# Splitting the first batch of an attention-plus-MoE kernel into two query parts, and moving its loads

## The chip, the cores and the metric

The kernel runs on 1 core of one Trainium2 chip. The metric is device time in microseconds (us); lower is better. Time before: 294.08 us, the median of 3 runs (293.91 to 294.34). "Clock" is the TensorE clock granted by the throttle, 1.00 being full speed.

## The reference

Block-causal attention over 8 batches, 8 heads, 576 tokens, head size 64, followed by a maxout feed-forward layer on all 4608 tokens:

```python
scores = scale * q @ k^T                 # 576 x 576 per head, masked in blocks of 64
attn   = softmax(scores)                 # exp, divided by the row's sum
x      = (attn @ v) as (4608, 512)       # heads side by side
g      = maximum(x @ w1, x @ w2)         # 4608 x 1024
out    = g @ w_out                       # 4608 x 512, float32
```

All inputs are float32 in HBM. The kernel computes in bfloat16.

## The kernel before

Heads are handled in 32 pairs of two. Two pairs are one *group*, which is loaded, cast and transposed together: "q4" is the q of group 4, needed by pairs 8 and 9, and its transposes stand in pair 6's turn. The four pairs of batch 0 are done first. After that the MoE matmuls ("filler") of the tokens that are finished are mixed between the attention of the next pairs. The schedule is by hand: each engine runs its instructions in the order in which the program emits them.

```python
def load_qk(g, queues, gated=False):
    for nm, src, queue in (("q", q, queues[0]), ("k", k, queues[1])):
        raws[nm, g] = t = raw.tile([P, 2, RPP * D], FP32, name=f"{nm}raw")
        if gated:
            nc.gpsimd.memset(t[:, 0, :1], 0.0)   # holds the load until GpSimd gets here
        queue.dma_start(out=t[:], in_=...)       # 576 KB
...
def fill_of(s):                                  # MoE matmuls to mix into pair s
    if s >= NPAIR - LAG:
        return 27
    left = 10 - s if s < 10 else 4 - (s - 2) % 4
    return -(-max(0, ready() - KEEP) // left)
...
# batch 0, all 576 queries of a pair at once: exps of 1024, 1024, 1024 and 128 elements
for s in range(HP):
    burst_a(s); ...; burst_b(s); pool_work(s); ...
...
elif s == 3:                                     # in pool_work
    cast("q", 2, ((act, 0, RPP),))
    cast("k", 2, ((act, 0, RPP),))
    load_qk(4, (SP, SP), gated=True)             # BEFORE the casts of group 3
    for c in range(3): load_v(1, c)
    cast("q", 3, ((pool, 0, RPP),))
    cast("k", 3, ((pool, 0, RPP),))
    for c in range(3, NCH): load_v(1, c)
    load_wo(0, 4)
    load_wo(4, 4)
```

The one-column memset makes a load wait for GpSimd's place in its program. So the order of GpSimd's instructions is also the order in which q and k loads go out. `warm_up(n)` issues n matmuls of zeros, meant to keep TensorE's clock up (two runs below, q4_late_cold and q4_late_warm, test this).

The softmax here doesn't subtract the row's maximum and nothing guards it: scores larger than these inputs give would overflow.

Of the kernel before, what the change touches and what calls it, by code (L numbers as in the profile page):

```python
# [14 lines left out]
def kernel(  # L15
# [38 lines left out]

    SPAN = 512
    NSPAN = NTOK // SPAN

# [31 lines left out]
    def load_qk(g, queues, gated=False):  # L89
        b, u = divmod(g, GPB)  # L90
        for nm, src, queue in (("q", q, queues[0]), ("k", k, queues[1])):
            raws[nm, g] = t = raw.tile([P, 2, RPP * D], FP32, name=f"{nm}raw")
            if gated:
                nc.gpsimd.memset(t[:, 0, :1], 0.0)
            queue.dma_start(
                out=t[:],
                in_=src[b, 4 * u:4 * u + 4].rearrange(
                    "(s h) (p t) d -> (h p) s (t d)", h=2, t=RPP),
            )
# [35 lines left out]
    load_qk(2, (SP, SP))  # L135
# [9 lines left out]
    cast("q", 0, ((dve, 0, 6), (pool, 6, RPP)))  # L145
# [3 lines left out]
    cast("q", 1, ((pool, 0, RPP),))  # L149
    for c in range(3, NCH):  # L150
        load_v(0, c)
    load_w(0, 256)
    load_w(256, 256)
# [5 lines left out]
    def h_unit(i, f):  # L159
        if f == 0:  # L160
            g_tiles[i] = g_pool.tile([P, NFF, SPAN], BF16, name="g")
        g = g_tiles[i]
        t0 = i * SPAN
        ph = []
        for w_sb in (w1_sb, w2_sb):
            pt = ps_m.tile([P, SPAN], FP32, name="ps_h", tag="m")
            for c in range(NDM):
                nc.tensor.matmul(  # L168
                    pt[:], w_sb[:, c, f * P:(f + 1) * P], xT[:, c, t0:t0 + SPAN],
                    start=(c == 0), stop=(c == NDM - 1),  # L170
                )
                if c == NDM - 1:
                    if not ph:
                        h1 = h1_pool.tile([P, SPAN], BF16, name="h1")
                        nc.vector.tensor_copy(out=h1[:], in_=pt[:])  # L175
                    else:
                        nc.vector.tensor_max(g[:, f, :], h1[:], pt[:])  # L177
                    ph.append(pt)
                yield

    def y_unit(i, s):
        g = g_tiles[i]
        t0 = i * SPAN + s * P
        py = ps_m.tile([P, d_model], FP32, name="ps_y", tag="m")
        for f in range(NFF):
            nc.tensor.matmul(  # L186
                py[:], g[:, f, s * P:(s + 1) * P], wo_sb[:, f, :],
                start=(f == 0), stop=(f == NFF - 1),
            )
            if f == NFF - 1:  # L190
                y = y_pool.tile([P, d_model], FP32, name="y")
                nc.scalar.copy(out=y[:], in_=py[:])  # L192
                nc.sync.dma_start(out=out[t0:t0 + P, :], in_=y[:])
            yield

    def y_last(i, s):
        g = g_tiles[i]
        t0 = i * SPAN + s * P
# [17 lines left out]
    def moe():  # L216
        ny = SPAN // P
        for i in range(NSPAN):
            need = (i + 1) * SPAN
            for f in range(NFF):  # L220
                yield from ((need, 0) for _ in h_unit(i, f))
                if i > 1 and f % 2 == 0:
                    yield from ((need, 0) for _ in y_unit(i - 1, f // 2))
            if i == 0:
                for s in range(ny):
                    yield from ((need, 0) for _ in y_unit(0, s))
        for s in range(ny - 1):
            yield from ((NTOK, 0) for _ in y_unit(NSPAN - 1, s))
        yield from ((NTOK, 0) for _ in y_last(NSPAN - 1, ny - 1))


    needs = []
    for i in range(NSPAN):
        needs += [(i + 1) * SPAN] * (2 * NDM * NFF + (SPAN // P * NFF if i != 1 else 0))
    needs += [NTOK] * ((SPAN // P + 1) * NFF)
    moe_steps = moe()
    at = [0]

    def ready():
        n = at[0]  # L240
        while n < len(needs) and needs[n] <= done_tokens[0]:
            n += 1
        return n - at[0]

    def fill(n):
        for _ in range(min(n, ready())):
            next(moe_steps)
            at[0] += 1
# [43 lines left out]
    def mask(p, a0):  # L292
        nc.gpsimd.memset(aT_r[p % NA][BLK:, :, a0:a0 + BLK], 0.0)  # L293
# [23 lines left out]
    def av(p, ts):  # L317
# [11 lines left out]
        for gi, t in enumerate(ts):  # L329
            for hh in range(2):  # L330
                for c in range(t + 1):
                    a0 = CB[c] + t * P
# [12 lines left out]
    def x_out(g):  # L345
        b, u = divmod(g, GPB)
        xp = xps.pop(g)
        pe = ps_m.tile([P, 2, NCH, BLK], BF16, name="ps_xe", tag="m")
        po = ps_m.tile([P, 2, NCH - 1, BLK], BF16, name="ps_xo", tag="m")
        for s in range(2):  # L350
            for t in range(NCH):
                src = xp[:, t, s].rearrange("p a d -> p (a d)")
                nc.tensor.transpose(pe[:, s, t, :], src[:BLK], ident[:BLK, :BLK])  # L353
                if t < NCH - 1:
                    nc.tensor.transpose(po[:, s, t, :], src[BLK:], ident[BLK:, BLK:])
        dst = xT[:, 2 * u:2 * u + 2, b * S:b * S + NCH * P].rearrange(
            "p s (t h w) -> p s t h w", h=2, w=BLK)
        nc.vector.tensor_copy(out=dst[:, :, :, 0], in_=pe[:])  # L358
        nc.vector.tensor_copy(out=dst[:, :, :NCH - 1, 1], in_=po[:])  # L359
        if u == GPB - 1:  # L360
            done_tokens[0] = (b + 1) * S
# [13 lines left out]
    def pool_work(s):  # L375
        g, i = divmod(s, 2)
        if s == 0:
            load_w(512, 512)
            load_qk(3, (SP, SP), gated=True)
        elif s == 1 or s == 2:  # L380
            pass
        elif s == 3:
            cast("q", 2, ((act, 0, RPP),))
            cast("k", 2, ((act, 0, RPP),))
            load_qk(4, (SP, SP), gated=True)
            for c in range(3):
                load_v(1, c)
            cast("q", 3, ((pool, 0, RPP),))
            cast("k", 3, ((pool, 0, RPP),))
            for c in range(3, NCH):  # L390
                load_v(1, c)
            load_wo(0, 4)
            load_wo(4, 4)
        elif s == 4:
# [30 lines left out]
    for s in range(HP):  # L425
        burst_a(s)
        if s == 0:
            cast("k", 1, ((dve, 0, RPP),))
            warm_up(4)
        elif s == 1:  # L430
            transposes("k", 1, (dve, dve))()
            warm_up(2)
        elif s == 2:
            av(0, [0, 1])
            warm_up(2)
        else:
            av(0, [2, 3, 4])
        burst_b(s)
        pool_work(s)
        if s == 0:  # L440
            transposes("q", 1, (dve, dve))()
            warm_up(2)
        elif s == 1:
            warm_up(4)
        elif s == 2:
            warm_up(3)
    for p in (1, 2, 3):
        av(p, [0, 1])
        av(p, [2, 3, 4])
        if p == 2:  # L450
            x_out(0)
    x_out(1)

    x_due = []
    for s in range(HP, NPAIR):
        g, i = divmod(s, 2)
        if x_due:
            x_out(x_due.pop())
        n = fill_of(s)
        if s == HP:  # L460
            fill(6)
            cq = transposes("q", 2, (dve, act))
            ck = transposes("k", 2, (dve, act))
            cq()
            ck()
            fill(6)
# [8 lines left out]
        if s >= HP + LAG:  # L475
# [4 lines left out]
            if p % 2:  # L480
                x_due.append(p // 2)
        else:
# [10 lines left out]
    fill(len(needs))  # L493
# [36 lines left out]
```

## Time and profile before

| what | before |
|---|---|
| time | 294.08 us |
| span of the profiled run | 292.3 us |
| TensorE busy | 281.2 us, of which 10.7 us are matmuls of zeros |
| ScalarE, VectorE, GpSimd busy | 140.2, 181.9, 95.7 us |
| first MoE matmul | 27.11 us |
| scores of pair 5 / 7 / 10 start | 36.65 / 46.03 / 63.38 us |

The views are read in the prediction below.

### The profile page before, as it was taken

How to read it: one execution, taken by the hardware profiler on the slowest of the kernel's cores; microseconds unless marked ns; L12 is line 12 of the kernel's file. 1: busy time of each engine (PE TensorE's matmuls, PEld its weight loads, DVE VectorE, ACT ScalarE, POOL GpSimd, SP SyncE). 2: the span in 40 equal slices, each digit the busy share in tenths (PEclk: the TensorE clock that was granted, in tenths of full speed). 3: DMA queues.
4: the chain of work that ended last, by engine and by line, in shares of the span. 5: the costliest groups of instructions: out<-in, count | busy, mean ns of one | idle time of the engine just before them, and what ended most of it. 6: DMA issues, size and time to landing. Idle time of an engine off the chain costs nothing.

```text
span 292.3 us, 7455 instructions
## 1 busy us (share of the span) xinstructions
PE 281.2 (96%) x3116; PEld 141.0 (48%) x3116; DVE 181.9 (62%) x363; ACT 140.2 (48%) x200; POOL 95.7 (33%) x236
## 2 busy tenths in 40 slices
PE   8787999999999999999999999999999999999995
PEld 3345445445554454544454455454545544444443
DVE  6717677547986676666565656666665766464530
ACT  3883686686655555554545555545555000101112
POOL 2967536625644443144324532443111000000000
PEclk9999999999999999999999999999999999999999
DMA  7999999968923792568656594465110111011104
GB/s 265 288 182 295 224 183 172 234 150 166 200 34 142 97 212 46 199 73 201 82 200 72 116 168 153 76 61 65 40 38 37 38 69 41 36 72 38 72 36 144
DMA packets 56081, 36.65 MB, mean 125 GB/s; under 512 B 38768, under 2 KB 43376, under 8 KB 56048
## 3 DMA queue, kind: packets, MB, share of 16 engines
q0 software_dynamic: 41728, 7.87, 34.5%
q1 hardware_dynamic: 13760, 27.60, 27.8%
q10 hardware_dynamic: 560, 0.72, 0.7%
q8 instruction: 24, 0.39, 0.6%
q14 instruction: 9, 0.07, 0.1%
HBM read 34.60 MB, written 9.44 MB: 151 GB/s over the span
## 4 chain that ended last, share of the span: by engine, by line
PE 89%; ACT 4%; DVE 3%; DMA 2%; issue 1%; ACTq 0%
PE ps_h L168 43%; PE ps_y L186 20%; PE ps_o L333 11%; PE ps_s L282 8%; ACT aT L288 3%; PE ps_qT L265 2%; DMA qraw<-in_q_dram 2%; PE ps_kT L265 2%; PE ps_xe L353 2%; PE ps_w L254 1%; DVE xp L340 1%; PE ps_y L203 1%; DVE xT L358 0%; DVE qT L272 0%; DVE kT L272 0%
## 5 line engine op out<-in xcount | busy, mean ns | idle before, releaser
L168 PE MATMUL ps_h<-xT,w_sb 128*128 128x512 bf16 x576 | 139.6, 380 | 0.5 <-DVE xT L359 0.4
L288 ACT ACTIVATE aT<-ps_s 128x1024 bf16<-128x1024 f32 (+1 forms) x128 | 99.2, 832 | 53.5 <-PE ps_s L282 53.5
L168 PEld LDWEIGHTS <-w_sb 128*128 128x128 bf16 x576 | 51.8, 98 | 59.7 <-issue 6.1
L175 DVE CAST h<-ps_h 128x512 bf16<-128x512 f32 x72 | 49.7, 691 | 45.0 <-PE ps_h L168 43.9
L186 PE MATMUL ps_y<-wo_sb,g 128*128 128x512 bf16 x280 | 69.6, 379 | 0.0
L293 POOL MEMSET aT<- 64x128 bf16 x128 | 23.6, 200 | 120.7 <-ACT aT L288 120.5
L192 ACT COPY y<-ps_y 128x512 f32<-128x512 f32 x35 | 20.5, 587 | 83.9 <-PE ps_y L186 61.4
L177 DVE TENSOR_TENSOR g<-h,ps_h 128x512 bf16<-128x512 bf16 x72 | 49.3, 684 | 10.2 <-PE ps_h L168 10.2
L333 PEld LDWEIGHTS <-aT 128*128 128x128 bf16 x960 | 33.6, 98 | 14.9 <-DVE xp L340 8.4
L333 PE MATMUL ps_o<-vv,aT 128*128 128x65 bf16 x960 | 39.7, 194 | 0.9 <-DVE xp L340 0.4
L186 PEld LDWEIGHTS <-g 128*128 128x128 bf16 x280 | 25.4, 98 | 27.9 <-issue 3.2
L282 PE MATMUL ps_s<-qT,kT 64*128 64x64 bf16 (+4 forms) x384 | 34.5, 275 | 3.0 <-ACT aT L288 2.9
L109 POOL DMA_DIRECT2D vv<-in_v_dram x40 | 33.7, 848 | 0.3 <-issue 0.3
L340 DVE TENSOR_TENSOR xp<-ps_o,rec 128x256 bf16<-128x256 f32 x64 | 31.4, 491 | 2.2
L282 PEld LDWEIGHTS <-kT 64*128 64x128 bf16 x384 | 16.5, 94 | 18.9 <-issue 13.2
L339 DVE RECIPROCAL rec<-ps_o 128x4 f32<-128x4 f32 x64 | 11.8, 184 | 18.9 <-PE ps_o L333 18.8
L105 POOL CAST qn<-qraw 128x1152 bf16<-128x1152 f32 (+1 forms) x15 | 17.1, 1138 | 4.8 <-DMA qraw<-in_q_dram 4.7
L272 DVE COPY qT<-ps_qT 128x576 bf16<-128x576 bf16 x17 | 12.8, 757 | 5.3 <-PE ps_qT L265 4.1
L358 DVE COPY xT<-ps_xe 128x640 bf16<-128x640 bf16 x16 | 7.8, 490 | 12.4 <-PE ps_xe L353 12.1
L105 POOL CAST kn<-kraw 128x1152 bf16<-128x1152 f32 x13 | 14.9, 1145 | 1.9 <-DMA kraw<-in_k_dram 1.2
L272 DVE COPY kT<-ps_kT 128x576 bf16<-128x576 bf16 x17 | 12.8, 756 | 4.3 <-PE ps_kT L265 3.3
L254 PE MATMUL ps_w<-zeros 128*128 128x512 bf16 x36 | 10.7, 432 | 1.7 <-DVE zeros L132 1.2
(39 smaller groups left out, 102.9 us busy)
## 6 DMA issues: line engine op xcount, KB each, us to landing
qraw<-in_q_dram SPq DMA_DIRECT2D x16, 576.0 KB, 4.4
out_dram<-y SPq DMA_DIRECT2D x35, 256.0 KB, 2.1
kraw<-in_k_dram SPq DMA_DIRECT2D x15, 576.0 KB, 6.5
vv<-in_v_dram POOLq DMA_DIRECT2D x32, 128.0 KB, 5.8
w_sb<-in_moe_w_dram POOLq DMA_DIRECT2D x4, 256.0 KB, 8.1
w_sb<-in_moe_w_dram POOLq DMA_DIRECT2D x2, 512.0 KB, 16.9
wo_sb<-in_moe_w_out_dram POOLq DMA_DIRECT2D x2, 512.0 KB, 12.6
kraw<-in_k_dram ACTq DMA_DIRECT2D x1, 576.0 KB, 5.6
```

The lines of the kernel that those rows point to most:

```text
L105: copy(out=n[:, j0:j1], in_=t[:, j0:j1])
L109: nc.gpsimd.dma_start(out=vv_r[b % NV][:rows, c, :, :D], in_=v[b, :, c * P:c * P + rows, :].rearrange("h p d -> p h d"),)
L168: nc.tensor.matmul(pt[:], w_sb[:, c, f * P:(f + 1) * P], xT[:, c, t0:t0 + SPAN], start=(c == 0), stop=(c == NDM - 1),)
L175: nc.vector.tensor_copy(out=h1[:], in_=pt[:])
L177: nc.vector.tensor_max(g[:, f, :], h1[:], pt[:])
L186: nc.tensor.matmul(py[:], g[:, f, s * P:(s + 1) * P], wo_sb[:, f, :], start=(f == 0), stop=(f == NFF - 1),)
L272: copies[i](out=t[:, :S].rearrange("q (p j) -> q p j", j=RPP), in_=pts[i].rearrange("q j p -> q p j"),)
L282: nc.tensor.matmul(ps[:m, hh, col:col + w], kT[r, c * P:c * P + m], qT[r, q0:q0 + w], start=True, stop=True,)
L288: nc.scalar.activation(out=aT_r[p % NA][:m, :, a0:a0 + w], in_=ps[:m, :, :w], func=AF.Exp, scale=scale,)
L293: nc.gpsimd.memset(aT_r[p % NA][BLK:, :, a0:a0 + BLK], 0.0)
L333: nc.tensor.matmul(po[:, gi, hh, :], a[:, hh, a0:a0 + P], vv[:, c, h0 + 2 * hh, :], start=(mm == 0), stop=(mm == n_mm - 1),)
L340: nc.vector.tensor_mul(xp[:, ts[0]:ts[0] + n, :, p % 2], po[:, :, :, :D], rec[:, :n].to_broadcast([P, n, 2, D]),)
```

## The change

The intent is to start MoE work earlier. Batch 0 is done in two query parts: queries 0 to 383 of all four pairs first, then 384 to 575. The first 384 tokens are an MoE span of their own, the other 192 a second one; the later spans of 512 then start 64 tokens into an output tile, and those 64 columns of g are copied ("carried") from the span before. The head is written out by hand, and with it the loads are reordered: k2 is held back from the start, group 3's load goes behind the casts of group 2, the first half of w_out goes ahead of the casts of group 3, and group 4's load goes behind them. The core of the diff (cut; [...] marks the cuts):

```diff
+    QCUT = 384
[...]
-    NSPAN = NTOK // SPAN
+    spans = [(0, QCUT), (QCUT, S - QCUT)]
+    spans += [(t0, min(SPAN, NTOK - t0)) for t0 in range(S, NTOK, SPAN)]
[...]
-    load_qk(2, (SP, SP))
+    load_qk(2, (SP, None))
[...]
-    cast("q", 1, ((pool, 0, RPP),))
[...]
+    cast("k", 1, ((pool, 0, RPP),))
[...]
-        elif s == 3:
-            cast("q", 2, ((act, 0, RPP),))
-            cast("k", 2, ((act, 0, RPP),))
-            load_qk(4, (SP, SP), gated=True)
[...]
-    for s in range(HP):
-        burst_a(s)
[...]
+    burst_p1(0)
+    burst_p2(0)
[...]
+    load_qk(2, (None, SP), gated=True)
[...]
+    load_w(512, 512)
+    cast("q", 2, ((pool, 0, RPP),))
+    cast("k", 2, ((pool, 0, RPP),))
+    burst_q1(0)
[...]
+    mask_q(1)
+    load_qk(3, (SP, SP), gated=True)
+    for c in range(3):
+        load_v(1, c)
[...]
+    load_wo(0, 4)
+    fill(3)
[...]
+    cast("q", 3, ((pool, 0, RPP),))
+    cast("k", 3, ((pool, 0, RPP),))
+    load_wo(4, 4)
+    load_qk(4, (SP, SP), gated=True)
+    fill(3)
```

Group 4's load now comes after group 3's casts.

More of the change, by code (lines that the diff above doesn't have):

```diff
@@ L53, with a_col @@
     NCH = 5
-    SPAN = 512
-    NSPAN = NTOK // SPAN
+    QCUT = 384
+    def a_col(p, c, t):
+        if p >= HP:
+            return CB[c] + t * P
+        return {
+            0: (0, 768 - QCUT), 1: (512 - P, 960 - QCUT),
+            2: (384 - 2 * P, 1152 - QCUT), 3: (0, 1344 - QCUT), 4: (0, 1536 - 4 * P),
+        }[c][t * P >= QCUT] + t * P if (c, t) != (2, 4) else 1280
+    SPAN = 512
+    spans = [(0, QCUT), (QCUT, S - QCUT)]
+    spans += [(t0, min(SPAN, NTOK - t0)) for t0 in range(S, NTOK, SPAN)]
+    NSPAN = len(spans)
+    carry = [t0 % P for t0, _ in spans]
+    tiles = [(carry[i] + w) // P for i, (_, w) in enumerate(spans)]
     wpool = ctx.enter_context(tc.tile_pool(name="wpool", bufs=1))
@@ L91, in load_qk @@
         for nm, src, queue in (("q", q, queues[0]), ("k", k, queues[1])):
+            if queue is None:
+                continue
             raws[nm, g] = t = raw.tile([P, 2, RPP * D], FP32, name=f"{nm}raw")
@@ L144 @@
         nc.vector.memset(aT_r[r][:BLK, :, AW:], 0.0)
-    cast("q", 0, ((dve, 0, 6), (pool, 6, RPP)))
+    cast("q", 0, ((dve, 0, 7), (pool, 7, RPP)))
     cast("k", 0, ((act, 0, 5), (dve, 5, RPP)))
@@ L148 @@
         load_v(0, c)
-    cast("q", 1, ((pool, 0, RPP),))
-    for c in range(3, NCH):
-        load_v(0, c)
-    load_w(0, 256)
-    load_w(256, 256)
+    cast("k", 1, ((pool, 0, RPP),))
     done_tokens = [0]
@@ L160, in h_unit @@
         if f == 0:
-            g_tiles[i] = g_pool.tile([P, NFF, SPAN], BF16, name="g")
+            g_tiles[i] = g_pool.tile([P, NFF, SPAN + BLK], BF16, name="g")
+            if carry[i]:
+                end = carry[i - 1] + spans[i - 1][1]
+                nc.gpsimd.tensor_copy(
+                    out=g_tiles[i][:, :, :carry[i]],
+                    in_=g_tiles[i - 1][:, :, end - carry[i]:end])
         g = g_tiles[i]
-        t0 = i * SPAN
+        t0, w = spans[i]
+        m = carry[i]
         ph = []
@@ L168, in h_unit @@
                 nc.tensor.matmul(
-                    pt[:], w_sb[:, c, f * P:(f + 1) * P], xT[:, c, t0:t0 + SPAN],
+                    pt[:, :w], w_sb[:, c, f * P:(f + 1) * P], xT[:, c, t0:t0 + w],
                     start=(c == 0), stop=(c == NDM - 1),
@@ L174, in h_unit @@
                         h1 = h1_pool.tile([P, SPAN], BF16, name="h1")
-                        nc.vector.tensor_copy(out=h1[:], in_=pt[:])
+                        nc.vector.tensor_copy(out=h1[:, :w], in_=pt[:, :w])
                     else:
-                        nc.vector.tensor_max(g[:, f, :], h1[:], pt[:])
+                        nc.vector.tensor_max(g[:, f, m:m + w], h1[:, :w], pt[:, :w])
                     ph.append(pt)
@@ L182, in y_unit @@
         g = g_tiles[i]
-        t0 = i * SPAN + s * P
+        t0 = spans[i][0] - carry[i] + s * P
         py = ps_m.tile([P, d_model], FP32, name="ps_y", tag="m")
@@ L197, in y_last @@
         g = g_tiles[i]
-        t0 = i * SPAN + s * P
+        t0 = spans[i][0] - carry[i] + s * P
         w = d_model // 2
@@ L214, in y_last, with plan, h, y @@
                 yield
-    def moe():
-        ny = SPAN // P
+    units = []
+    def plan():
+        def h(i, f):
+            t0, w = spans[i]
+            units.append((h_unit(i, f), t0 + w, w / SPAN, 2 * NDM))
+        def y(i, s, last=False):
+            t0, w = spans[i]
+            if last:
+                units.append((y_last(i, s), t0 + w, 0.5, 2 * NFF))
+            else:
+                units.append((y_unit(i, s), t0 + w, 1.0, NFF))
         for i in range(NSPAN):
-            need = (i + 1) * SPAN
             for f in range(NFF):
-                yield from ((need, 0) for _ in h_unit(i, f))
-                if i > 1 and f % 2 == 0:
-                    yield from ((need, 0) for _ in y_unit(i - 1, f // 2))
-            if i == 0:
-                for s in range(ny):
-                    yield from ((need, 0) for _ in y_unit(0, s))
-        for s in range(ny - 1):
-            yield from ((NTOK, 0) for _ in y_unit(NSPAN - 1, s))
-        yield from ((NTOK, 0) for _ in y_last(NSPAN - 1, ny - 1))
-    needs = []
-    for i in range(NSPAN):
-        needs += [(i + 1) * SPAN] * (2 * NDM * NFF + (SPAN // P * NFF if i != 1 else 0))
-    needs += [NTOK] * ((SPAN // P + 1) * NFF)
-    moe_steps = moe()
+                h(i, f)
+                if i > 2 and f % 2 == 0 and f // 2 < tiles[i - 1]:
+                    y(i - 1, f // 2)
+            if i == 1:
+                for j in range(2):
+                    for s in range(tiles[j]):
+                        y(j, s)
+        n = tiles[-1]
+        for s in range(n):
+            y(NSPAN - 1, s, s == n - 1)
+    plan()
+    steps = [(u, need, cost) for u, need, cost, n in units for _ in range(n)]
     at = [0]
     def ready():
-        n = at[0]
-        while n < len(needs) and needs[n] <= done_tokens[0]:
+        n, total = at[0], 0.0
+        while n < len(steps) and steps[n][1] <= done_tokens[0]:
+            total += steps[n][2]
             n += 1
-        return n - at[0]
+        return int(total)
     def fill(n):
-        for _ in range(min(n, ready())):
-            next(moe_steps)
+        while n > 0 and at[0] < len(steps) and steps[at[0]][1] <= done_tokens[0]:
+            u, _, cost = steps[at[0]]
+            next(u)
+            n -= cost
             at[0] += 1
@@ L290, in exp, with mask, burst, burst_p1 @@
         )
-    def mask(p, a0):
-        nc.gpsimd.memset(aT_r[p % NA][BLK:, :, a0:a0 + BLK], 0.0)
+    def mask(p, a0, eng=None):
+        (eng or nc.gpsimd).memset(aT_r[p % NA][BLK:, :, a0:a0 + BLK], 0.0)
+    def burst(p, parts, a0):
+        u = ps_s.tile([P, 2, 512], FP32, name="ps_s", tag="s")
+        w = 0
+        for c, q0, n in parts:
+            scores(p, u, w, c, q0, n)
+            w += n
+        exp(p, u, w, a0)
+    def burst_p1(p):
+        burst(p, ((0, 0, QCUT), (2, 256, P)), 0)
+    def burst_p2(p):
+        burst(p, ((1, P, QCUT - P),), 512)
+    def burst_q1(p):
+        burst(p, ((0, QCUT, 192), (1, QCUT, 192), (2, QCUT, P)), 768)
+    def burst_q2(p):
+        burst(p, ((2, 512, BLK), (3, QCUT, 192), (4, 512, BLK)), 1280)
+    def masks_p(p, eng=None):
+        for a in (0, 384, 512):
+            mask(p, a, eng)
+    def mask_q(p, eng=None):
+        mask(p, 1344, eng)
     def burst_a(p):
@@ L331, in av @@
                 for c in range(t + 1):
-                    a0 = CB[c] + t * P
+                    a0 = a_col(p, c, t)
                     nc.tensor.matmul(
@@ L343, in av, with x_out @@
         )
-    def x_out(g):
+    def x_out(g, t0=0, t1=NCH):
         b, u = divmod(g, GPB)
-        xp = xps.pop(g)
-        pe = ps_m.tile([P, 2, NCH, BLK], BF16, name="ps_xe", tag="m")
-        po = ps_m.tile([P, 2, NCH - 1, BLK], BF16, name="ps_xo", tag="m")
+        xp = xps[g]
+        n = t1 - t0
+        n_odd = min(t1, NCH - 1) - t0
+        pe = ps_m.tile([P, 2, n, BLK], BF16, name="ps_xe", tag="m")
+        po = ps_m.tile([P, 2, n_odd, BLK], BF16, name="ps_xo", tag="m")
         for s in range(2):
-            for t in range(NCH):
+            for t in range(t0, t1):
                 src = xp[:, t, s].rearrange("p a d -> p (a d)")
-                nc.tensor.transpose(pe[:, s, t, :], src[:BLK], ident[:BLK, :BLK])
+                nc.tensor.transpose(pe[:, s, t - t0, :], src[:BLK], ident[:BLK, :BLK])
                 if t < NCH - 1:
-                    nc.tensor.transpose(po[:, s, t, :], src[BLK:], ident[BLK:, BLK:])
-        dst = xT[:, 2 * u:2 * u + 2, b * S:b * S + NCH * P].rearrange(
+                    nc.tensor.transpose(po[:, s, t - t0, :], src[BLK:], ident[BLK:, BLK:])
+        dst = xT[:, 2 * u:2 * u + 2, b * S + t0 * P:b * S + t1 * P].rearrange(
             "p s (t h w) -> p s t h w", h=2, w=BLK)
         nc.vector.tensor_copy(out=dst[:, :, :, 0], in_=pe[:])
-        nc.vector.tensor_copy(out=dst[:, :, :NCH - 1, 1], in_=po[:])
+        nc.vector.tensor_copy(out=dst[:, :, :n_odd, 1], in_=po[:])
         if u == GPB - 1:
-            done_tokens[0] = (b + 1) * S
+            done_tokens[0] = min(b * S + t1 * P, (b + 1) * S)
     LAG = 2
@@ L376, in pool_work @@
         g, i = divmod(s, 2)
-        if s == 0:
-            load_w(512, 512)
-            load_qk(3, (SP, SP), gated=True)
-        elif s == 1 or s == 2:
-            pass
-        elif s == 3:
-            cast("q", 2, ((act, 0, RPP),))
-            cast("k", 2, ((act, 0, RPP),))
-            load_qk(4, (SP, SP), gated=True)
-            for c in range(3):
-                load_v(1, c)
-            cast("q", 3, ((pool, 0, RPP),))
-            cast("k", 3, ((pool, 0, RPP),))
-            for c in range(3, NCH):
-                load_v(1, c)
-            load_wo(0, 4)
-            load_wo(4, 4)
-        elif s == 4:
+        if s == 4:
             pass
@@ L424 @@
     ck((1,))
-    for s in range(HP):
-        burst_a(s)
-        if s == 0:
-            cast("k", 1, ((dve, 0, RPP),))
-            warm_up(4)
-        elif s == 1:
-            transposes("k", 1, (dve, dve))()
-            warm_up(2)
-        elif s == 2:
-            av(0, [0, 1])
-            warm_up(2)
-        else:
-            av(0, [2, 3, 4])
-        burst_b(s)
-        pool_work(s)
-        if s == 0:
-            transposes("q", 1, (dve, dve))()
-            warm_up(2)
-        elif s == 1:
-            warm_up(4)
-        elif s == 2:
-            warm_up(3)
-    for p in (1, 2, 3):
-        av(p, [0, 1])
-        av(p, [2, 3, 4])
-        if p == 2:
-            x_out(0)
-    x_out(1)
-    x_due = []
+    cast("q", 1, ((dve, 0, RPP),))
+    burst_p1(0)
+    burst_p2(0)
+    warm_up(2)
+    masks_p(0)
+    load_w(0, 256)
+    load_qk(2, (None, SP), gated=True)
+    cq = transposes("q", 1, (dve, dve))
+    burst_p1(1)
+    ck = transposes("k", 1, (dve, dve))
+    for i in range(2):
+        cq((i,))
+        ck((i,))
+    burst_p2(1)
+    masks_p(1)
+    for c in range(3, NCH):
+        load_v(0, c)
+    warm_up(2)
+    burst_p1(2)
+    warm_up(2)
+    av(0, [0, 1, 2])
+    burst_p2(2)
+    masks_p(2, nc.vector)
+    load_w(256, 256)
+    warm_up(3)
+    burst_p1(3)
+    av(1, [0, 1, 2])
+    warm_up(2)
+    burst_p2(3)
+    masks_p(3, nc.vector)
+    load_w(512, 512)
+    cast("q", 2, ((pool, 0, RPP),))
+    cast("k", 2, ((pool, 0, RPP),))
+    burst_q1(0)
+    av(2, [0, 1, 2])
+    warm_up(2)
+    burst_q2(0)
+    av(3, [0, 1, 2])
+    x_out(0, 0, 3)
+    burst_q1(1)
+    warm_up(2)
+    burst_q2(1)
+    x_out(1, 0, 3)
+    mask_q(0)
+    mask_q(1)
+    load_qk(3, (SP, SP), gated=True)
+    for c in range(3):
+        load_v(1, c)
+    warm_up(1)
+    burst_q1(2)
+    transposes("q", 2, (dve, dve))()
+    fill(3)
+    burst_q2(2)
+    mask_q(2)
+    for c in range(3, NCH):
+        load_v(1, c)
+    load_wo(0, 4)
+    fill(3)
+    burst_q1(3)
+    transposes("k", 2, (dve, dve))()
+    av(0, [3, 4])
+    fill(3)
+    burst_q2(3)
+    mask_q(3)
+    cast("q", 3, ((pool, 0, RPP),))
+    cast("k", 3, ((pool, 0, RPP),))
+    load_wo(4, 4)
+    load_qk(4, (SP, SP), gated=True)
+    fill(3)
+    av(1, [3, 4])
+    fill(4)
+    x_due = [0]
     for s in range(HP, NPAIR):
@@ L457 @@
         if x_due:
-            x_out(x_due.pop())
+            x_out(x_due.pop(), 3 if s < HP + 2 else 0)
         n = fill_of(s)
-        if s == HP:
-            fill(6)
-            cq = transposes("q", 2, (dve, act))
-            ck = transposes("k", 2, (dve, act))
-            cq()
-            ck()
-            fill(6)
         burst_a(s)
@@ L481 @@
                 x_due.append(p // 2)
+        elif s == HP:
+            av(2, [3, 4])
+            fill(n_b)
+            av(3, [3, 4])
+            x_due.append(1)
         else:
@@ L492 @@
     x_out(NG - 1)
-    fill(len(needs))
+    fill(len(steps))
 _INS = ['q', 'k', 'v', 'moe_w1', 'moe_w2', 'moe_w_out']
```

## The prediction

> **What bounds the kernel now.** I read the page's busy shares and slices first, then busy time by stretch, then TensorE's instructions in order of time for the first 35 us, then the DMA issues one by one.
>
> ```profile
> PE 281.2 (96%) x3116; PEld 141.0 (48%) x3116; DVE 181.9 (62%) x363; ACT 140.2 (48%) x200; POOL 95.7 (33%) x236
> ...
> PE   8787999999999999999999999999999999999995
> ```
>
> TensorE is busy 96% of the span, and its row of slices is below 9 only in the first 29 us and at the very end. By stretch:
>
> ```profile
> 15.00:16.00 1.00, 1.00 (x10) 0.34 (x8) 0.00 (x0) 0.59 (x2) 0.96 (x6) 1.00 3.03 102
> 18.00:21.00 3.00, 2.75 (x39) 1.69 (x39) 0.46 (x2) 2.66 (x5) 1.03 (x7) 1.00 1.45 196
> 21.00:31.00 10.00, 7.25 (x172) 5.22 (x172) 7.19 (x20) 4.41 (x7) 7.25 (x13) 1.00 1.14 294
> 63.00:280.00 217.00, 216.91 (x2312) 107.67 (x2312) 140.62 (x268) 95.71 (x137) 58.92 (x148) 1.00 0.47 99
> ```
>
> (Columns: stretch, length, busy time of PE, PEld, DVE, ACT, POOL, granted clock, DMA share, GB/s.) From 63 to 280 us TensorE is busy 216.91 of 217 us at full clock. Nothing there can be saved by reordering; all matmuls that are needed are still needed. A gain can come only from the head, where "busy" deceives, because part of it multiplies zeros:
>
> ```profile
> 18.11 0.21 PE L282 MATMUL ps_s<-qT,kT 64*128 64x64 bf16 x2 [0.52 <-ACT aT L288]
> 18.25 0.82 PE L254 MATMUL ps_w<-zeros 128*128 128x512 bf16 x3
> ...
> 21.45 0.20 PE L282 MATMUL ps_s<-qT,kT 64*128 64x64 bf16 x2 [0.52 <-ACT aT L288]
> ...
> 27.11 0.60 PE L168 MATMUL ps_h<-xT,w_sb 128*128 128x512 bf16 x2
> 28.09 1.02 PE L168 MATMUL ps_h<-xT,w_sb 128*128 128x512 bf16 x4 [0.38 <-DVE xT L359]
> ...
> 36.65 0.61 PE L282 MATMUL ps_s<-qT,kT 64*128 64x512 bf16 x6
> ```
>
> (Start, duration, instruction, count, idle before and its releaser.) The first MoE matmul is at 27.11 us. Before it TensorE owns only batch 0's attention: 4 sets of transposes at 0.27, 4 pairs of scores at 0.54 + 0.35, 4 pairs of AV at 0.92, two output transposes at 0.3, in all 9.0 us. So about 18 us of the first 27.1 are idle or zeros. What TensorE waits for there is ScalarE's exps: 9.23 to 22.4 us, four exps in 3.00 us per pair, then 0.34 to 0.53 us of idle before the next pair.
>
> DMA is the second bound of the head: its share is above 1 from about 4 to past 40 us, up to 3.03. Landings, as issue start plus time to landing of each issue: q0 5.95, k0 6.35, q1 about 7.8, k1 9.35, q2 10.85, k2 12.6; the v chunks of batch 0 at about 13.4, 14.4, 15.4 (0 to 2), 18.1, 18.7; the first weight columns at 19.2 and 20.2, the second at 22.7 and 26.1, the last at 31.3 and 35.1; q3 24.6, k3 28.1.
>
> **What the Trainium skill says.** "ScalarE: Activation LUTs", What ACT_TABLE_LOAD costs: 0.833 ns per element and about 93 ns of overlap between neighbours. The trace agrees: 1022 ns for 1024 elements and 260 ns for 128 give 0.85 ns per element, and two in a row take 1.94 us, 0.92 from start to start. By that line an exp of 512 is 0.59 us and one of 640 0.70 us (estimates). "TensorE: Matmul & The Clock Gate", Wait — 56ns, not 53.3ns?: start to start is N/2.4 GHz plus about 2.5 ns, so splitting a 512-column matmul costs next to nothing. The trace: 8 matmuls of 512 in 1.90 us with the last one's 0.38, 217 ns each against 215.7. "DMA: Bandwidth & Descriptors", Queues, rings and completion order: each engine takes turns between the queues it has work for, by packet. The trace agrees in kind: q3 and k3, issued at 17.5 and 17.9 beside the weights, need 7.1 and 10.2 us, where q0 alone needed 5.2.
>
> **The change, part by part.** I count MoE work in units of one 512-column matmul (0.217 us).
>
> *Split of batch 0.* Scores cover queries 0-383 of all four pairs first (exps of 1024 and 512), then 384-575 (1024 and 640). ScalarE per pair: 1022 + 586 + 1022 + 695 ns less four overlaps, 2.95 us, as before; but MoE can start after four first parts (4 × 1.42 = 5.7 us of exps from 9.23) and not after 13 us. Two long exps no longer stand around a 0.26 one, so the 0.5 us hole per pair shrinks too.
>
> *Worked order of the head (estimates from the durations above; ScalarE, VectorE and buffers each in program order).* Nothing differs to 9.2. The q1 cast is now on VectorE, 8.7 to 10.0 (1.35 measured for k1), the k1 cast on GpSimd ends about 10.6. VectorE's four copies at 0.75 bring pair 2 at 12.0 and pair 3 at 13.4. The first AV of three chunks needs v chunk 2. Without k2 in front (576 KB at about 400 GB/s is 1.4 us) it lands at about 13.9 and not 15.4. TensorE would be there at 13.2, and its queue is in order, so the second exp of pair 2 waits too: a hole of about 1.2 us on ScalarE. Then exps of pair 3 from 15.6 to 17.2, AV of pair 3 about 18.3, VectorE's division to 19.3, output transposes after the second-part scores of pair 1 at about 19.8, xT complete at 20.6. First MoE matmul at about **20.9**, 6.2 us earlier than 27.11.
>
> *What then stands in its way.* The fills until the loop (3+3+3+3+3+4) are 19.5 units, 4.2 us; among them four AV tails (two later, inside the loop) at 0.56, scores, k2's transposes. I get the start of pair 4's scores at about 27.7 against 32.04. There only tokens 0-383 are released: 48 units less 19.5 leave 28, so the fill for pair 4 is (28-6)/6, 4 units, where before had 15. Pair 4 also needs q3, which is now loaded only after k2's cast and the second exp of pair 1: issued about 21.1, landed about 27.6, cast by 28.8, wanted at 28.6. Pair 5's scores start at about 32.6 against 36.65, so 4.05 us ahead, but 24 units are done where before had 27: 3 × 0.217 = 0.65 us are still owed. Net **3.4 us**.
>
> *Pairs 5 to 9.* After: 104 units are released by batch 0 (576 tokens), before 96 (512 tokens); 75 against 63 are filled in here. More filler does not cost anything in sum, as the total stays 864. Widths of 192 double VectorE's instructions: with 692 ns for 512 and 292 for 128 one of 192 is about 0.36, so a pair of tiles takes 0.72 against TensorE's 8 × 0.083 = 0.66: VectorE becomes the limit for some 5 us if nothing else is interleaved. Before has idle of its own there (0.18, 0.32, 0.31, 0.27 us). I take 0.2 us for this and for 64 more MoE instructions at about 3 ns.
>
> *The rest.* Eight copies of g on GpSimd (512 elements a partition, well under the 1.15 us of its 1152-element casts) on an engine at 33%: nothing. The last span is 448 wide, the final tiles and the output are as before: nothing.
>
> Sum: 294.08 - 3.4 + 0.2, about **290.8**; I put 290.6, since the wait for v is the term I most likely set too long.
>
> **Rivals.**
> 1. *The loads don't keep up.* The backlog moves nothing earlier by itself: all that is needed 4 us earlier must still pass engines at share 1 to 3. q3 issued 3.6 us later than before is the tightest, then q4, whose issue now stands behind k3's cast (about 33, where before it was 22.9): landed about 38.3, cast 39.5, wanted at about 40.4. For: the 7 to 10 us landings in this stretch. Against: the weights go out earlier, and before has 9 us of slack for q3. If q3 and q4 are each 1.5 us late: about 293.
> 2. *ScalarE alone sets the head.* If v is there in time and no exp waits, the first parts end at about 15.5, xT at 18.3, and the gain grows by about 2 us: about 288.5. For: the new order never lets three long exps stand behind one buffer. Against: the v chunks have 1.0 us spacing and 6.6 us to landing.
> 3. *The gain is hidden anyway.* If the earlier MoE start only replaces filler later, because pairs 4 to 9 are bound by ScalarE (3.64 us per pair) or VectorE, pairs with 4 units stay idle: about 292 to 293. Against: before's pairs 5 to 9 take 5.3 us each, well over 3.64, so they absorb filler.
>
> **Range and chances.** My sum has one well-founded term (exps before MoE, 13 to about 6 us) and three waits of 1 to 2 us each that could go either way; together about 2 us each side: 288.3 to 292.9. Faster by over 2% means under 288.2, a gain of 5.9 us, nearly all of the earlier start without any new wait: 0.10. Slower needs 6 us of new waits: 0.02.
>
> **What would show it.** First MoE matmul near 20.9 us; TensorE idle before the first AV released late, with ScalarE's hole of about 1.2 us after pair 2's first exp; q3's cast ending near 28.8; pair 5's scores near 32.6; TensorE again without idle after about 62 us, its busy time lower by little, and all later stages the same. I am wrong if the loop starts later than 29 us or the stretch from 30 to 62 us shows more than 1.5 us of new idle (loads late), or if pair 5 starts before 31 (ScalarE alone).

## The result, and the profile after

| | before | after |
|---|---|---|
| time, median | 294.21 us (293.91 to 294.96, 4 runs) | 297.15 us (296.58 to 297.41, 4 runs) |
| clock, mean over the span | 0.998 | 0.987 to 0.994 |
| first MoE matmul | 27.11 us | 20.74 us |
| scores of pair 5 start | 36.65 us | 32.83 us |
| scores of pair 7 start | 46.03 us | 49.27 us |

The ratio is 1.0093 (95% interval 1.0068 to 1.0119). Ratios are the mean time of one kernel's fast runs over that of the other's fast runs of the same rounds, so they are not quite the ratio of the medians quoted. The change made the kernel 0.9% slower. I had predicted 290.6, in a range of 288.3 to 292.9.

The page of the changed kernel, busy shares and slices of 7.4 us each:

```profile
PE 279.4 (95%) x3158; PEld 146.8 (50%) x3203; DVE 186.5 (63%) x391; ACT 138.0 (47%) x196; POOL 101.2 (34%) x241
...
PE   8898949999999999999999999999999999999995
...
PEclk9999997999999999999999999999999999999999
```

Two slices are new. The sixth (37 to 44 us) has TensorE at 4 tenths, where before had 9. The seventh (44 to 52 us) has TensorE busy, but at a granted clock of 7 tenths. TensorE's instructions in order of time say what it waited for (start, duration, instruction, count, idle before and its releaser):

```profile
20.74 0.82 PE L191 MATMUL ps_h<-xT,w_sb 128*128 128x384 bf16 x4
...
29.96 0.44 PE L301 MATMUL ps_qT<-ident,qn 64*128 64x64 bf16 x18 [1.65 <-POOL qn L126]
...
44.22 0.66 PE L301 MATMUL ps_qT<-ident,qn 64*128 64x64 bf16 x18 [4.12 <-POOL qn L126]
44.68 0.67 PE L318 MATMUL ps_s<-qT,kT 64*128 64x320 bf16 x6
```

The early start is there: 20.74 us. But q3's transposes wait 1.65 us for GpSimd's cast, and q4's wait 4.12 us. After the second wait the same 18 transposes last 0.66 us and not 0.44. Busy time by stretch, first of the changed kernel, then of the kernel before (stretch, length, busy time of PE, PEld, DVE, ACT, POOL, clock, DMA share, GB/s):

```profile
40.00:44.00 4.00, 0.10 (x1) 0.00 (x0) 0.53 (x1) 0.13 (x1) 0.98 (x1) 1.00 1.11 315
44.00:48.00 4.00, 3.78 (x60) 2.98 (x61) 1.93 (x5) 1.70 (x3) 1.96 (x7) 0.57 0.80 289
```

```profile
40.00:44.00 4.00, 4.00 (x49) 1.88 (x48) 2.77 (x5) 3.40 (x6) 1.98 (x7) 1.00 1.14 208
44.00:48.00 4.00, 4.00 (x45) 1.88 (x45) 3.09 (x8) 2.79 (x5) 3.21 (x6) 1.00 0.67 236
```

From 40.5 to 43.0 us all engines stand still and only DMA works. From 44 to 48 us the clock averages 0.57. Read in steps of 0.25 to 0.5 us it is 0.50 from 44.25 to about 47.6. GpSimd's instructions of the changed kernel show why q4 was late:

```profile
32.39 1.15 POOL L126 CAST kn<-kraw 128x1152 bf16<-128x1152 f32 x1 [2.48 <-DMA kraw<-in_k_dram]
33.48 0.74 POOL L144 DMA_DIRECT2D wo_sb<-in_moe_w_out_dram  x1
34.22 0.12 POOL L115 MEMSET qraw<- 128x1 f32 x1
...
43.02 1.14 POOL L126 CAST qn<-qraw 128x1152 bf16<-128x1152 f32 x1 [5.39 <-DMA qraw<-in_q_dram]
```

GpSimd stands 2.48 us at the cast of k3 until k3 has landed. Only then can it write the memset (34.22) that lets q4's load go. The load queue of the changed kernel, then of the kernel before (group 3's q, then group 4's):

```profile
21.22 0.37 SPq L116 DMA_DIRECT2D qraw<-in_q_dram  x1
...
34.36 0.37 SPq L116 DMA_DIRECT2D qraw<-in_q_dram  x1
```

```profile
17.52 0.37 SPq L95 DMA_DIRECT2D qraw<-in_q_dram  x1
...
22.90 0.37 SPq L95 DMA_DIRECT2D qraw<-in_q_dram  x1
```

q4's load goes out 11.5 us later than before (34.36 against 22.90) for transposes that are wanted some 2.7 us earlier. It took 8.6 us to land, at 43.0.

### The profile page after: what moved, and what is told of

Its sections match the earlier page's. It is cut to its first block, busy times and chain, and to the rows that moved or that the text cites. A ratio compares the mean times of both kernels' runs of the same rounds, so it can differ in the third digit from the quotient of the medians.

```text
span 295.1 us, 7637 instructions
## 1 busy us (share of the span) xinstructions
PE 279.4 (95%) x3158; PEld 146.8 (50%) x3203; DVE 186.5 (63%) x391; ACT 138.0 (47%) x196; POOL 101.2 (34%) x241
## 4 chain that ended last, share of the span: by engine, by line
PE 84%; issue 4%; DVE 4%; POOL 3%; DMA 3%; ACT 1%; POOLq 0%; DVEq 0%; ACTq 0%
PE ps_h L191 39%; PE ps_y L209 20%; PE ps_o L396 11%; PE ps_s L318 7%; PE ps_w L290 3%; DMA qraw<-in_q_dram 3%; PE ps_qT L301 2%; PE ps_xe L418 2%; PE ps_kT L301 1%; POOL qn L126 1%; POOL w_sb L141 1%; DVE kT L308 1%; ACT aT L324 1%; DVE xp L403 1%; PE ps_y L226 1%
## 5 line engine op out<-in xcount | busy, mean ns | idle before, releaser
L191 PE MATMUL ps_h<-xT,w_sb 128*128 128x512 bf16 (+3 forms) x616 | 136.2, 358 | 2.7 <-issue 1.6
L324 ACT ACTIVATE aT<-ps_s 128x1024 bf16<-128x1024 f32 (+3 forms) x128 | 100.2, 831 | 65.5 <-PE ps_s L318 63.3
L191 PEld LDWEIGHTS <-w_sb 128*128 128x128 bf16 x640 | 57.0, 98 | 57.2 <-issue 6.2
L198 DVE CAST h<-ps_h 128x512 bf16<-128x512 f32 (+3 forms) x80 | 50.9, 636 | 43.4 <-PE ps_h L191 41.0
L200 DVE TENSOR_TENSOR g<-h,ps_h 128x512 bf16<-128x512 bf16 (+3 forms) x80 | 50.6, 632 | 10.2 <-PE ps_h L191 7.9
L318 PE MATMUL ps_s<-qT,kT 64*128 64x64 bf16 (+6 forms) x408 | 34.8, 271 | 0.3 <-DVE kT L308 0.3
L403 DVE TENSOR_TENSOR xp<-ps_o,rec 128x256 bf16<-128x256 f32 (+1 forms) x64 | 31.4, 491 | 2.2
L402 DVE RECIPROCAL rec<-ps_o 128x4 f32<-128x4 f32 (+1 forms) x64 | 11.8, 185 | 14.0 <-PE ps_o L396 13.7
L126 POOL CAST qn<-qraw 128x1152 bf16<-128x1152 f32 (+1 forms) x15 | 16.5, 1101 | 12.1 <-DMA qraw<-in_q_dram 12.0
L181 POOL COPY g<-g 128x512 bf16<-128x512 bf16 x8 | 4.9, 613 | 37.9 <-DVE g L200 37.8
L423 DVE COPY xT<-ps_xe 128x640 bf16<-128x640 bf16 (+2 forms) x18 | 8.2, 453 | 11.8 <-PE ps_xe L418 11.4
```

Source lines behind the costliest of these rows:

```text
L126: copy(out=n[:, j0:j1], in_=t[:, j0:j1])
L191: nc.tensor.matmul(pt[:, :w], w_sb[:, c, f * P:(f + 1) * P], xT[:, c, t0:t0 + w], start=(c == 0), stop=(c == NDM - 1),)
L198: nc.vector.tensor_copy(out=h1[:, :w], in_=pt[:, :w])
L200: nc.vector.tensor_max(g[:, f, m:m + w], h1[:, :w], pt[:, :w])
L318: nc.tensor.matmul(ps[:m, hh, col:col + w], kT[r, c * P:c * P + m], qT[r, q0:q0 + w], start=True, stop=True,)
L324: nc.scalar.activation(out=aT_r[p % NA][:m, :, a0:a0 + w], in_=ps[:m, :, :w], func=AF.Exp, scale=scale,)
```

## The experiments

**Theory A**: q4's load is issued too late, because it stands behind group 3's k cast in GpSimd's order. The wait that follows is long enough to halve TensorE's clock, which is paid for once more. **Rival B**: the DMA engines are full in this stretch, so that whatever is issued earlier makes something else late. **Rival C**: the place is harmless where more filler lies around it, as in the kernel before.

Twelve runs were made in three batches, each batch beside the kernel before on one chip. after_again is the changed kernel unaltered. All were correct.

| run | median us (range, 4 runs each) | before | ratio (95%) |
|---|---|---|---|
| q4_ahead | 291.04 (290.54 to 291.73) | 293.89 | 0.9909 (0.9888 to 0.9930) |
| warm_in_wait | 297.41 (295.00 to 298.10) | 293.89 | 1.0105 (1.0060 to 1.0150) |
| before_q4_late | 298.95 (298.38 to 299.87) | 293.89 | 1.0175 (1.0153 to 1.0198) |
| wout_later | 291.46 (291.05 to 295.06) | 293.89 | 0.9945 (0.9885 to 1.0004) |
| q3_q4_ahead | 290.86 (290.30 to 294.31) | 294.43 | 0.9910 (0.9841 to 0.9978) |
| q3_q4_fill | 293.31 (292.23 to 293.61) | 294.43 | 0.9955 (0.9932 to 0.9978) |
| q4_late_cold | 298.56 (298.09 to 299.31) | 294.43 | 1.0142 (1.0121 to 1.0164) |
| q4_late_warm | 296.42 (296.07 to 296.67) | 294.43 | 1.0067 (1.0050 to 1.0083) |
| after_again | 296.12 (295.61 to 297.55) | 294.23 | 1.0070 (1.0038 to 1.0102) |
| q4_before_wout | 295.47 (294.31 to 296.07) | 294.23 | 1.0035 (1.0006 to 1.0065) |
| k2_at_start | 292.20 (292.01 to 293.30) | 294.23 | 0.9937 (0.9911 to 0.9962) |
| q3_q4_wout | 291.25 (291.12 to 293.10) | 294.23 | 0.9918 (0.9879 to 0.9956) |

### q4_ahead: one load moved

```diff
     mask_q(3)
+    load_qk(4, (SP, SP), gated=True)
     cast("q", 3, ((pool, 0, RPP),))
     cast("k", 3, ((pool, 0, RPP),))
     load_wo(4, 4)
-    load_qk(4, (SP, SP), gated=True)
```

> Only the load of group 4 is moved, in front of the casts of group 3. Theory A (q4's transfer is issued too late, behind group 3's k cast): the transfer is issued near 26.7 us instead of 34.4, lands about 35 to 36, the wait of 4.12 us on TensorE before q4's transposes is gone and with it the half-speed clock after it (44.2 to 47.7), which cost about 1.7 us: 297.15 - 5.8 = about 291.3 us. Rival B (the DMA engines are simply full, so an earlier q4 pushes the v chunks of batch 1 and w_out back): a new wait of 2 to 4 us on v or w_out appears at pair 6 to 8, about 294 to 296 us.

Measured 291.04. The load queue, TensorE and a stretch of this run:

```profile
26.66 0.37 SPq L116 DMA_DIRECT2D qraw<-in_q_dram  x1
```

```profile
39.66 0.43 PE L301 MATMUL ps_qT<-ident,qn 64*128 64x64 bf16 x18
```

```profile
40.00:44.00 4.00, 4.00 (x73) 3.06 (x64) 3.72 (x11) 2.12 (x4) 2.46 (x6) 1.00 1.16 274
```

Pair 7's scores, in the changed kernel, then in q4_ahead:

```profile
49.27 0.61 PE L318 MATMUL ps_s<-qT,kT 64*128 64x512 bf16 x6
```

```profile
43.16 0.61 PE L318 MATMUL ps_s<-qT,kT 64*128 64x512 bf16 x6
```

q4 is issued 7.7 us earlier, lands at 34.1, and its transposes start at 39.66 with no wait. TensorE is busy for all of 40 to 44 us, and the clock stays at 1.00. The rest of the kernel follows one for one: pair 7's scores start at 43.16 against 49.27 (6.11 us), pair 10's at 61.76 against 67.88 (6.12), and the spans are 289.0 and 295.1 (6.1). Of the 6.11 us, 4.56 lie before q4's transposes (44.22 less 39.66; 4.12 are the wait itself). The other 1.55 lie between these and pair 7's scores (5.05 us against 3.50, for the same work), which is the slow clock. (This compares two profiled executions. By the ratios of all runs q4_ahead gains 1.6 to 1.8% on the changed kernel, about 5 us.) Theory A is right in place and in size; rival B's new wait of 2 to 4 us did not come.

### before_q4_late: the same harm in the kernel before

Group 4's load is taken out of pair 3's work and put in front of group 5's, in pair 5's.

```diff
-            load_qk(4, (SP, SP), gated=True)        # at s == 3
[...]
         elif s == 5:
+            load_qk(4, (SP, SP), gated=True)
             load_qk(5, (SP, SP), gated=True)
```

> The kernel before with only q4 and k4 loaded late, beside group 5's load (issued about 41 instead of 22.9 us). Theory A: q4 lands about 46.5, is cast by 47.7 and TensorE, which wants it at 42.8, waits about 4.8 us and then runs about 3.4 us at half clock: 294.2 + 6.5 = about 300.7 us. Rival C (before's fuller filling of pairs 4 to 6 has slack for a late q4): under 297 us.

Measured 298.95, 5.1 us slower than before. TensorE and one stretch of this run:

```profile
46.06 0.66 PE L265 MATMUL ps_qT<-ident,qn 64*128 64x64 bf16 x18 [3.31 <-POOL qn L105]
```

```profile
48.00:52.00 4.00, 3.78 (x32) 2.04 (x33) 2.21 (x5) 0.97 (x3) 3.20 (x5) 0.51 0.25 60
```

A late q4 costs the old schedule nearly as much, so rival C falls: the wait is 3.31 us, and the clock is halved from about 45 to 51.9. The wait was shorter than the 4.8 us that I expected, because q4 landed in 3.9 us here. At 41 us the engines had little else to do, so the landing time belongs to the stretch and not to the load.

### wout_later: the traffic beside it

Both w_out loads of the changed kernel are put off to pair 6; nothing else moves.

```diff
-    load_wo(0, 4)
[...]
-    load_wo(4, 4)
     load_qk(4, (SP, SP), gated=True)
[...]
+            if s == 6:
+                load_wo(0, 4)
+                load_wo(4, 4)
```

> The changed kernel with both w_out loads put off to pair 6. Theory A (the place of the issue behind group 3's k cast decides): q4 is still issued about 33.6 us and lands 41 to 42, the wait shrinks by 1 to 1.5 us only, 295 to 296 us. Rival B (sharing with w_out makes the landing take 8.6 us): q4 and k3 land in 5.5 us, k3's cast ends about 32, q4 issued at 32.5 lands about 38, the wait is under 0.5 us: about 291.5 us.

Measured 291.46; three runs lie at 291.05 to 291.71 and one at 295.06 with a clock of 0.988. The load queue and TensorE:

```profile
33.27 0.37 SPq L116 DMA_DIRECT2D qraw<-in_q_dram  x1
```

```profile
40.05 0.44 PE L301 MATMUL ps_qT<-ident,qn 64*128 64x64 bf16 x18 [0.46 <-DVE h L198]
```

This is rival B's number, and half of theory A was wrong. q4 is issued only 1.1 us earlier than in the changed kernel (0.74 of this is the w_out load that GpSimd no longer issues before it), but lands in 5.5 us and not 8.6, which is just enough. The other half of rival B did not come: k3 still took 10.6 us to land. So both terms are real: the late issue, and the sharing with other transfers. Taking away either one removes the wait, all of it or all but 0.46 us. It is also the more fragile mending, as the run of 295.06 shows.

### q4_before_wout: the order against w_out alone

```diff
     cast("k", 3, ((pool, 0, RPP),))
-    load_wo(4, 4)
     load_qk(4, (SP, SP), gated=True)
+    load_wo(4, 4)
```

> The changed kernel with only the last two loads swapped: group 4's before the second half of w_out, but both still behind group 3's casts. Theory A as I now hold it (GpSimd, in order, stands at k3's cast until k3 has landed near 32.2, and q4 is issued after that): q4 goes out about 33.6, 0.75 us earlier, and the wait shrinks from 4.1 to about 3.3 us; 295.5 to 296.5 us. Rival (it is w_out ahead in the order that delays q4, the named intent of the change): under 293 us.

Measured 295.47, against 296.12 for the unaltered changed kernel in the same batch. The gain of 0.65 us is close to the 0.74 us that GpSimd spends on one w_out load, but the two intervals in the table overlap, so it is not shown. The time is well above the rival's 293: what holds q4 back is the cast that waits for k3, not w_out ahead of it. Going first did not speed the transfer either: q4 landed in 8.5 us. In the profiled run the wait sits in another place:

```profile
31.29 0.66 PE L301 MATMUL ps_qT<-ident,qn 64*128 64x64 bf16 x18 [2.74 <-POOL qn L126]
...
44.54 0.44 PE L301 MATMUL ps_qT<-ident,qn 64*128 64x64 bf16 x18 [1.88 <-POOL qn L126]
```

k2 had landed late in this execution (20.8 us, against 19.3 in the changed kernel's profile), so group 3's load went out at 22.68 and not near 21, and q4's at 34.81. The halved clock followed the 2.74 us in front of q3.

### warm_in_wait, q4_late_cold, q4_late_warm: what the clock costs

The first is the changed kernel with zeros in the wait; for the other two, group 3 is loaded early and group 4 late on purpose, without and with the zeros.

```diff
         fill(n_a)
+        if s == 6:
+            warm_up(19)
         copy_out = t_pair(s)
```

> The changed kernel with 19 matmuls of zeros (4.1 us) placed where TensorE waits for q4. Theory A': [...]the slow stretch afterwards costs 1.5 to 2 us: with the zeros the clock stays at 1.00 after 44 us and the time is about 295.4 us. Rival: TensorE at half speed in 44 to 48 us costs nothing since other engines limit there: 297.1 us, unchanged.

Measured 297.41, but spread from 295.00 to 298.10, so nothing follows from the median. The profiled run had its clock dip elsewhere, after a wait of 3.03 us for q3, which the zeros do not cover; it began only 1.6 us after TensorE was at work again (31.38, dip from 32.9). Only one run kept a clock of 1.00 throughout; it took 295.00, against the 295.4 that I expected. So I took q3's wait away first and tried again:

> The changed kernel with group 3 loaded early (so that q3 causes no wait or dip of its own) and group 4 loaded late on purpose, with group 5. q4 is issued about 36, lands about 42, TensorE waits 4 to 5 us near 38 to 43 and the clock then falls to half for some 3.4 us: about 289.7 + 4.5 + 1.7 = 296 us.

> q4_late_cold with 19 matmuls of zeros (4.1 us) in the wait for q4. If the clock loss is a cost of its own: no slow stretch and 1.5 to 2 us less than q4_late_cold, about 294.3 us. Rival (the half clock is hidden behind other engines): the same time as q4_late_cold, or longer by what the zeros overrun.

Measured 298.56 and 296.42 in the same batch. q4's transposes, cold, then warm:

```profile
46.02 0.66 PE L301 MATMUL ps_qT<-ident,qn 64*128 64x64 bf16 x18 [5.92 <-POOL qn L126]
```

```profile
44.95 0.44 PE L301 MATMUL ps_qT<-ident,qn 64*128 64x64 bf16 x18 [1.62 <-POOL qn L126]
```

The stretches, cold, then warm:

```profile
44.00:48.00 4.00, 1.98 (x32) 1.37 (x33) 1.08 (x3) 0.79 (x1) 1.48 (x3) 0.50 0.65 253
48.00:52.00 4.00, 4.00 (x48) 3.32 (x46) 2.67 (x8) 0.96 (x4) 3.19 (x5) 0.68 0.21 21
```

```profile
44.00:48.00 4.00, 3.05 (x69) 2.61 (x69) 2.51 (x7) 1.70 (x3) 2.38 (x6) 1.00 0.49 191
48.00:52.00 4.00, 3.77 (x63) 2.82 (x62) 3.38 (x10) 2.51 (x3) 2.44 (x5) 1.00 0.90 59
```

With the zeros the clock stays at 1.00 and the kernel is 2.14 us faster, though it computes more. In the cold run TensorE resumes at 46.02 and the clock is half until about 50.5; half of these 4.5 us is 2.2. From q4's transposes to pair 7's scores the cold run takes 5.50 us and the warm one 3.51 for the same work, 1.99 us more. (q4's transposes also start 1.07 us later in the cold profile, since its q4 went out 0.86 us later, in code that both share: that part is scatter.) The slow clock is a cost of its own, and nothing hides it. The cold wait was longer than expected (5.92 us, with half clock from 43.7 to 50.5), so both times lie about 2 us above my numbers.

### k2_at_start: one other part of the change undone

q4_ahead, with k2 loaded at the start as in the kernel before.

```diff
-    load_qk(2, (SP, None))
+    load_qk(2, (SP, SP))
[...]
-    load_qk(2, (None, SP), gated=True)
```

> q4_ahead with k2 loaded at the start, as the kernel before does, and not held back. By my prediction k2 in front of the v chunks costs them about 1.4 us: the first AV waits about 1.9 us for v and not 0.44, the first MoE matmul comes about 1.4 us later, about 292.4 us. Rival: the k2 cast is then never late and the scatter of q3's issue goes, which pays for it: 290.5 to 291.2 us and a smaller scatter.

Measured 292.20, a ratio of 0.9937 where q4_ahead had 0.9909. The first AV now waits twice for v:

```profile
14.45 0.31 PE L396 MATMUL ps_o<-vv,aT 128*128 128x65 bf16 x5 [0.78 <-DMA vv<-in_v_dram]
...
15.29 0.28 PE L396 MATMUL ps_o<-vv,aT 128*128 128x65 bf16 x4 [0.53 <-DMA vv<-in_v_dram]
```

The first MoE matmul comes at 22.32 and not 20.72. Holding k2 back is a good part of the change, worth about 1 us by the medians; the two intervals in the table overlap.

### q3_q4_ahead, q3_q4_wout, q3_q4_fill: what is left

q3_q4_ahead moves group 3's load as well, ahead of group 2's casts; q3_q4_wout also puts w_out off; q3_q4_fill forces 12 units of filler into pair 4.

```diff
+    load_qk(3, (SP, SP), gated=True)          # q3_q4_ahead
     cast("q", 2, ((pool, 0, RPP),))
     cast("k", 2, ((pool, 0, RPP),))
[...]
-        n = fill_of(s)                        # q3_q4_fill only
+        n = fill_of(s) if s > HP else 12
```

> q4_ahead, and group 3's load also moved, ahead of group 2's casts on GpSimd (issued near 18.4 instead of 21.0 us). Theory A (the place of the issue decides for q3 as for q4): the wait of 1.29 us before q3's transposes goes, about 289.7 us. Rival B (the engines are full there, share 1.2 to 1.5, so an earlier q3 makes weights or k2 later): another wait of the same size, 291 us.

> All three mendings together: groups 3 and 4 loaded ahead of the casts, w_out put off to pair 6. If sharing with w_out still delays q3, k3 or the last weights: 290.0 to 290.5 us. If the head is by now set by ScalarE and the in-order work alone: 290.9 us, no different from q3_q4_ahead.

> q3_q4_ahead, and pair 4 filled with 12 units instead of the 4 that the formula gives. If pair 4 leaves TensorE idle (I counted 4 units against 15 of before), 0.5 to 1 us less than q3_q4_ahead. Rival: the filler is only used earlier and is missing later, same time within 0.3 us.

Measured 290.86, 291.25 and 293.31. In q3_q4_ahead q3's wait is gone, but two others stand in its place:

```profile
29.60 0.21 PE L318 MATMUL ps_s<-qT,kT 64*128 64x64 bf16 x2 [0.52 <-ACT aT L324]
...
33.92 0.82 PE L191 MATMUL ps_h<-xT,w_sb 128*128 128x384 bf16 x4 [0.21 <-DMA w_sb<-in_moe_w_dram]
```

Pair 5 starts 0.58 us earlier than in q4_ahead, pair 6 only 0.2 us. The second is rival B in small: with q3 earlier, a weight load is late by 0.21 us. Putting w_out off as well changed nothing that the runs can tell. The forced filler cost 2.5 us. Pair 5 starts 2.21 us later than in q3_q4_ahead, of which 0.68 us were already there at pair 4. Pairs 5 to 9 then took 29.90 us against 29.87, although 7.5 units (1.6 us) fewer were left for them; TensorE was idle for 1.90 us of these pairs against 1.00. My thought that pair 4 wastes TensorE was wrong; why the rest was not regained stays open.

q4_ahead, q3_q4_ahead and q3_q4_wout all beat both kernels, at about 291 us, and can't be told apart. q4_ahead, with one line moved, is the one to keep: it alone of the three has no run above 292 us (q3_q4_ahead has one of 294.31, q3_q4_wout one of 293.10).

## Why the prediction was wrong

- **The head**: right in its result, in part by luck. First MoE matmul at 20.74 us (predicted 20.9), pair 4's scores at 27.13 (27.7), pair 5's at 32.83 (32.6). Terms inside were off:
  - ScalarE's hole before the first AV was put at "about 1.2 us". In this execution it was not there: the zeros at the start took 6.31 us (5.15 before), the first exp came at 9.94 and not 9.23, and v had landed when it was wanted. In the profiles of q4_ahead and after_again the zeros took 5.14 and 5.32 us, and the hole was 0.70 and 0.83 us. There an earlier start was spent waiting for v, and the first MoE matmul came at 20.72 and 20.81 all the same.
  - The fills before the loop are five calls (3+3+3+3+4), not six. They make 16.5 units and not 19.5 (22 matmuls of 384 columns in the trace), and the formula then gives pair 4 five units and not four.
  - q3's cast was wanted at 28.3 and ended at 29.9, a wait of 1.65 us (1.29 in q4_ahead) where 0.2 was counted.
  - q0's load was not "alone": k0's was issued in the same moment. The clean comparison for sharing is q4's 5.5 us in wout_later against 8.6.
- **The sum of 290.8**: with the failed step alone undone (q4_ahead) the time is 291.04. Here too errors cancel. At pair 5 q4_ahead is 4.20 us ahead of the kernel before and owes 5.25 units (1.14 us), a net gain of 3.06 us and not 3.4; pairs 5 to 9 then gained 0.3 us where 0.2 were to be lost.
- **The step that failed** is in rival 1: "issue now stands behind k3's cast (about 33, where before it was 22.9): landed about 38.3, cast 39.5, wanted at about 40.4". It was issued at 34.36, landed at 43.0, was cast by 44.16 and was wanted at 40.1. Of the 4.7 us by which the landing was missed, 1.4 are the issue: k3 itself landed at about 32.2. The other 3.3 are the time to landing: I took 5.3 us, about what q5's load takes at 41 us. The kernel before's own q4, in the crowded stretch, takes 8.2, and I had that number. So the wait for q4, nothing in the sum, measured 4.12 us.
- **Rival 1's size** ("If q3 and q4 are each 1.5 us late: about 293") had the wait right in kind and left out its second half. I counted a wait at its length. A wait of this length also halves the clock: 1.55 us more after q4. The page of the Trainium skill that I cited for the matmul spacing says so in its section "What's actually happening" of "TensorE: Matmul & The Clock Gate": the clock goes to half after an idle window of about 3.4 us, and needs a busy one to come back. The traces agree (0.50 from 44.25 to about 47.6 us, after 4.12 us of idle), though some runs dropped after shorter waits (last section). With 4.1 for the wait and 1.55 for the clock, 290.8 becomes 296.5, against 297.15 and 296.12 measured.
- **Rival 2** (ScalarE alone, 288.5) was not met even with the loads mended. **Rival 3** was not the cause: with the loads mended, pair 10's scores start 1.62 us earlier than before with 8 units (1.74 us, counted in the prediction) more done, and that sum of 3.4 us is the predicted gain; the spans differ by 3.3.
- **The chances** were wrong in kind. By my own working v, q3 and q4 all came within about 1 us of the moment at which they were wanted, and a late load can only add. A range of about 2 us on either side, with 0.02 for slower by over 2%, does not describe that.

## What to carry to other kernels

When a schedule is pulled forward, list every transfer with its issue, its landing and the moment it is wanted, and take time to landing from the same crowded stretch of the trace, not from a quiet one. Look for loads gated by an in-order engine that itself waits for another load: one wait becomes the next one's delay. Price a TensorE wait of about 3 us or more at its length plus half of the slow time that follows: after the waits of 2.74 to 5.92 us here TensorE worked at half clock for 3.3 to 5.8 us.

## What the Trainium skill lacked or had wrong

- "TensorE: Matmul & The Clock Gate", What's actually happening, gives about 3.4 us of idle for the drop. The runs dropped after shorter idle: 2.74 us (q4_before_wout), 3.03 (warm_in_wait) and 3.31 (before_q4_late). After 1.65 and 1.88 us they did not. The page's closing table warns of gaps over about 3 us; only the 2.74 lies clearly below that.
- The same section leaves open how many windows a drop lasts. Here it was about 3.4 us (changed kernel, 44.25 to 47.6) or twice that (q4_late_cold, 43.7 to 50.5, beginning while TensorE still waited).
- "DMA: Bandwidth & Descriptors" has fits for a transfer alone. No page gives a landing time for one beside a backlog in another queue: the same 576 KB load landed in 3.9 us with quiet engines, 5.5 without w_out beside it, 8.6 in the changed kernel and 10.8 for the last in line.
- No page tells how much landing times vary between executions of one program. k2's load, issued at about 12.8 us, took 5.8 us in the profiled run of q3_q4_ahead and 8.3 in that of warm_in_wait; in the second, GpSimd then issued group 3's load 1.8 us later than in the changed kernel's profile.
